# A fused attention and max-out FFN kernel: units issued from a table, state by a hardware queue, attention transposed by the DMA crossbar, token sums on two column halves

## The chip, the cores and the metric

One core of a Trainium2 chip. The metric is the device time of one execution in microseconds (us), lower is better. A program on one core has no second die to compare with, so a run counts as fast unless it is over 1.5% above the fastest run of the same kernel. In the profile PE is TensorE (matmuls), PEld its weight loads, DVE VectorE, ACT ScalarE, POOL GpSimd, SP the engine that issues hardware DMAs; SPq is SP's queue.

## The reference, cut to what matters

```python
# x: (B=8, H=8, S=512, D=64), state: (8, 8, 32, 64)
scores  = x @ state^T / 8 ;  a  = softmax(scores)  ; xread = a  @ state    # 512 tokens read the state
scores2 = state @ x^T / 8 ;  a2 = softmax(scores2) ; sread = a2 @ x        # 32 state rows read the tokens
z = concat([xread, sread], tokens) as (8*544, 512)
h = max(z@w1, z@w2, z@w3)                                                  # 512 -> 768, three ways
out = h @ w_out                                                            # 768 -> 512
```

## The kernel before: the parts that matter

All matmuls are bf16. The 512-token part never forms `xread`: a *pm unit* `m_unit(b, m)` multiplies the state of batch b into 128 columns of the three weights, and an *up* multiplies that product by the transposed attention aT. Each engine works through its instructions in the order in which they are issued, and that order is written by hand.

```python
def m_unit(b, m, eng0, eng1):       # a "pm unit": 8 matmuls in 64-row x 32-column tiles, 2 PSUM banks
    for hp in range(4):
        for par in range(2):
            mm(pm[par][hp*32:(hp+1)*32, 0:384], sbd[r0:r0+64, b, hp, par, :],
               W[r0:r0+64, :, hp, m*128:(m+1)*128], True, True, pos=(r0, hp*32))
    ...                             # two copies out of PSUM, engines eng0 and eng1
def permute_x(b, eng, ...):         # x in the order that the transposes need ("xn")
    ...
    if b >= 2:                      # from batch 2 on, the DMA crossbar transposes x ("xT")
        nc.sync.dma_start_transpose(out=xT, in_=xn)
def a_to_T(b, ...):                 # attention transposed on TensorE, copied out by DVE ("aT")
    ...
def state_reads(b):                 # sread; 16 matmuls of x, then the token sums
    ...
    for par in range(2):
        for j in range(4):
            mm(pd, ones_h[:, par, :], e[:, j, par, :, :], False, par == 1 and j == 3)  # 128 columns, half zero

# opening: idle matmuls (warm the clock), state, batches 0 to 2 - a hand-written list of calls
# then seven passes; pass t makes the outputs of one batch, the ups of the next,
# and (in the first five) scores, reads and aT of the one after it:
for what in 2 * "o u o u u M A u o u o u u M A u u M".split():   # o output half, u up, M pm unit, A attention
    ...
```

The loads go out on POOL's software queue, which casts f32 to bf16: state, x0, W[0:256], x1, W[256:512], and then, in two later groups, the rest.

The softmax here doesn't subtract the row's maximum and nothing guards it: scores larger than these inputs give would overflow.

## Time and profile before

| | before |
|---|---|
| median of 4 runs | 180.21 us (179.22 to 180.93) |
| span of the profiled run | 178.3 us, mean granted clock 0.971 |
| opening, up to the first output half of pass 1 | 57.9 us |
| five passes with attention | 86.0 us |
| the pass of the state rows | 13.05 us |
| last batch and the end | 21.4 us |

The boundaries are read from TensorE's timeline: a pass starts with its first output half (`po`). In the time-ordered chain of waits of the kernel before (start, duration, what):

```profile
31.25 1.90 POOL xn L121
33.17 14.81 DMA xT<-xn
48.03 0.64 PE ps L134 x16
```

x of batch 2 is permuted, crosses the crossbar in 14.8 us, and only then do its scores start. While it crosses, the loads of later batches run on the other queue. The DMA view of that stretch (38 to 45 us) gives packets, MB and share per queue, q0 being the loads and q1 the crossing:

```profile
q0 software_dynamic: 1607, 0.81, 87.2%
q1 hardware_dynamic: 1608, 0.41, 48.8%
```

The packet counts are nearly equal (1607 and 1608), which fits queues that take turns packet by packet; the packets of the crossing are half as large (0.41 MB against 0.81).

### The profile page before, as it was taken

What the parts mean: (1) busy time and instruction counts of PE and PEld (TensorE: products, weight loads), DVE (VectorE), ACT (ScalarE), POOL (GpSimd) and SP (SyncE); (2) the same over time, 40 slices, a digit from 0 to 9 for tenths busy, and PEclk for the clock granted to TensorE, in tenths of its full rate; (3) what the DMA queues carried; (4) which work ended last, traced back from release to release, by engine and by line L of the source; (5) the groups of instructions that cost most, each with busy time, mean ns of one, the idle gap of its engine ahead of it and who ended that gap; (6) DMA issues with size and microseconds to landing.
All of it is one profiled execution on the core that took longest, in us unless ns stands there. A gap on an engine that the chain in (4) does not pass through costs nothing.

```text
span 178.3 us, 3585 instructions
## 1 busy us (share of the span) xinstructions
PE 161.5 (91%) x1399; PEld 77.9 (44%) x1423; DVE 110.2 (62%) x195; ACT 98.4 (55%) x197; POOL 43.6 (24%) x47
## 2 busy tenths in 40 slices
PE   7958894999499999999999999999999999999880
PEld 2433452235235445444544454445444557754330
DVE  3258888388455459756975686668576764347800
ACT  2244673473446576577566847684767552444240
POOL 7909547400071062006200710170022000000000
PEclk9996999699969999999999999999999999999999
DMA  3999999999917326202620352053302022034032
GB/s 58 146 187 198 194 205 198 197 189 172 90 75 161 122 118 121 118 0 118 121 118 0 133 106 119 4 165 74 121 0 118 16 106 118 0 132 106 1 148 89
DMA packets 29473, 19.89 MB, mean 112 GB/s; under 512 B 13200, under 2 KB 26768, under 8 KB 29456
## 3 DMA queue, kind: packets, MB, share of 16 engines
q0 software_dynamic: 14000, 7.60, 32.0%
q1 hardware_dynamic: 15456, 12.06, 23.2%
q8 instruction: 11, 0.18, 0.4%
q14 instruction: 6, 0.05, 0.1%
HBM read 15.20 MB, written 8.91 MB: 135 GB/s over the span
## 4 chain that ended last, share of the span: by engine, by line
PE 65%; DMA 19%; DVE 5%; POOL 4%; issue 2%; ACT 1%; DVEq 0%; POOLq 0%
PE pw L134 28%; PE po L134 24%; DMA x_sb<-in_x_dram 11%; DMA xT<-xn 8%; PE pm L134 5%; PE pr L134 3%; PE ps L134 2%; DVE t L281 2%; PE pa L137 2%; POOL W L84 1%; POOL xn L121 1%; POOL a L233 1%; DVE ht L284 1%; PE px L137 1%; ACT xT L167 1%
## 5 line engine op out<-in xcount | busy, mean ns | idle before, releaser
L134 PE MATMUL pw<-aT,M_sb 128*128 128x512 bf16 x269 | 74.7, 388 | 3.4 <-DVE aT L207 2.3
L134 PE MATMUL po<-wout,ht 128*128 128x512 bf16 x200 | 54.6, 386 | 1.1 <-DVE ht L284 0.5
L281 DVE TENSOR_TENSOR t<-t,pw 128x512 bf16<-128x512 bf16 (+1 forms) x54 | 34.8, 644 | 22.4 <-PE pw L134 14.5
L167 ACT CAST M_sb<-pm 128x384 bf16<-128x384 f32 x88 | 38.0, 485 | 18.7 <-PE pm L134 18.7
L278 ACT CAST t<-pw 128x512 bf16<-128x512 f32 (+1 forms) x54 | 30.6, 566 | 22.8 <-PE pw L134 19.6
L134 PEld LDWEIGHTS <-M_sb 128*128 128x128 bf16 x288 | 26.9, 100 | 33.5 <-issue 4.8
L284 DVE TENSOR_TENSOR ht<-t,pw 128x512 bf16<-128x512 bf16 (+1 forms) x54 | 35.5, 658 | 7.6 <-PE pw L134 2.7
L233 POOL TENSOR_TENSOR a<-e,rden 128x512 bf16<-128x512 bf16 x16 | 16.6, 1041 | 91.5 <-DVE rden L232 91.5
L310 ACT COPY o<-po 128x512 f32<-128x512 f32 x33 | 19.4, 586 | 21.9 <-PE po L134 20.2
L134 PEld LDWEIGHTS <-ht 128*128 128x128 bf16 x204 | 18.9, 99 | 22.1 <-issue 3.2
L229 DVE TENSOR_REDUCE den<-e 128x16 f32<-128x512 bf16 x16 | 10.8, 675 | 14.5 <-ACT e L225 14.5
L134 PE MATMUL pm<-W,sbd 64*32 64x384 bf16 x384 | 17.3, 351 | 0.4 <-DMA W<-in_moe_w_dram 0.4
L134 PEld LDWEIGHTS <-sbd 64*32 64x32 bf16 x384 | 5.3, 90 | 18.9 <-issue 18.8
L121 POOL COPY xn<-x_sb 128x2048 bf16<-128x2048 bf16 x6 | 11.3, 1890 | 1.0 <-DMA x_sb<-in_x_dram 1.0
L225 ACT ACTIVATE e<-ps 128x512 bf16<-128x512 f32 x16 | 9.7, 612 | 2.2 <-PE ps L134 2.2
L134 PE MATMUL ps<-sbd,xT 128*128 128x64 bf16 x128 | 6.3, 194 | 3.8 <-DMA xT<-xn 2.3
L134 PE MATMUL pw<-AT,W 128*128 128x256 bf16 x72 | 9.2, 273 | 0.1
L253 DVE RECIPROCAL rd<-pr 128x128 f32<-128x128 f32 x8 | 7.6, 950 | 2.4 <-PE pr L134 1.8
L134 PE MATMUL pz<-zeros 128*128 128x512 bf16 x26 | 7.8, 448 | 1.2 <-DVE zeros L73 1.2
L134 PEld LDWEIGHTS <-W 128*128 128x128 bf16 x72 | 7.1, 98 | 2.5
L207 DVE COPY aT<-pa 128x1024 bf16<-128x1024 bf16 (+1 forms) x9 | 5.7, 631 | 3.4 <-PE pa L137 3.4
L134 PEld LDWEIGHTS <-xT 128*128 128x128 bf16 x128 | 4.6, 98 | 6.4 <-DMA xT<-xn 2.5
(37 smaller groups left out, 75.8 us busy)
## 6 DMA issues: line engine op xcount, KB each, us to landing
out_dram<-o SPq DMA_DIRECT2D x14, 512.0 KB, 2.6
x_sb<-in_x_dram POOLq DMA_DIRECT2D x8, 512.0 KB, 12.6
W<-in_moe_w_dram POOLq DMA_DIRECT2D x9, 256.0 KB, 7.8
out_dram<-o SPq DMA_DIRECT2D x4, 256.0 KB, 2.0
wout<-in_moe_w_out_dram POOLq DMA_DIRECT2D x1, 768.0 KB, 11.3
out_dram<-o SPq DMA_DIRECT2D x8, 64.0 KB, 1.7
st<-in_state_dram POOLq DMA_DIRECT2D x1, 256.0 KB, 3.8
xT<-xn SPq DMA_TRANSPOSE x6, 5.3
```

Source lines behind the costliest of these rows:

```text
L121: eng.tensor_copy(out=x_nat[b][:, k * n:(k + 1) * n], in_=x_sb[:, b, :, k * n:(k + 1) * n].rearrange("p h j d -> p j h d"))
L134: nc.tensor.matmul(out_ap, lhsT, rhs, start=start, stop=stop, tile_position=pos)
L167: nc.scalar.copy(out=o, in_=i)
L207: nc.vector.tensor_copy(out=d["aT"][:, :, j0 * 128:j1 * 128], in_=pa)
L225: nc.scalar.activation(out=e.rearrange("p j a hp n -> p (j a hp n)"), in_=ps.rearrange("p j a hp n -> p (j a hp n)"), func=AF.Exp, scale=s ...
L229: nc.vector.reduce_sum(out=den, in_=ef, axis=AX.X)
L233: nc.gpsimd.tensor_mul(out=d["a"][:, j0:j0 + 2].rearrange("p j a hp n -> p (j a hp) n"), in0=ef, in1=rden.unsqueeze(2).to_broadcast((128, ...
L253: nc.vector.reciprocal(out=rd, in_=pd.rearrange("p (hp n) -> p hp n", hp=HP))
L278: nc.scalar.copy(out=t[:, :nn], in_=pw[:, :nn])
L281: nc.vector.tensor_max(t[:, :nn], hts[g, "t"][:, :nn], pw[:, :nn])
L284: nc.vector.tensor_max(hts[g][:, m, :nn], hts[g, "t"][:, :nn], pw[:, :nn])
L310: nc.scalar.copy(out=o[:, j % 2, :], in_=po)
```

## The change

Its intent: fewer stalls of TensorE in the opening, and less work for TensorE in the passes. The core of the diff, cut:

```diff
+OPENING = """
+id, idle 9, sel, idle 9, lx 0, lw 0 1, lx 1, pm 0 0 v, lw 4 6, pm 0 1 g, lw 1 2, ...
+... u 0 1 0, pm 2 - g, aT 1 - v, xb 2, u 0 1 1, ... u 1 4 0, lx 7, pm 3 - g, u 1 1 0,
+lx 6, u 1 0 1, ... xb 3, u 1 4 2, ... u 1 5 1, lx 4, u 1 5 2, o 0 0 0 a, o 0 0 1 a, u 1 2 1, S 2 1 g,
+S 2 0 g, ab 2, u 1 3 1, o 0 1 0 v, M 2 2 aa, R 1, ... R 2, lx 5
+"""       # lx/lw: loads, pm: permute x, xb/ab: crossbar of x/attention, xT/aT: the same on TensorE,
+          # S: scores, M: pm unit, u: up, o: output half, R: state reads; last letters: engine
+PERIOD = "o o u u u u S S o o M M m u R u o u o X u u u u u u u P u u o u o u m M M"
-    nc.gpsimd.dma_start(out=st16, in_=state)              # software queue, casts
+    nc.sync.dma_start(out=st32, in_=state)                # hardware queue, f32
+    nc.scalar.copy(out=st16, in_=st32)
-            for j in range(J):
-                mm(pd, ones_h[:, par, :], e[:, j, par, :, :], False, par == 1 and j == J - 1)
+        for j in range(J):
+            for par in range(2):
+                mm(pd[par*64:par*64+64], ones, e[:, j, par, :, :], False, j == J - 1, pos=(0, par*64))
+    def a_crossbar(b):                                    # batches 2 to 7
+        nc.sync.dma_start_transpose(out=aT(b), in_=a_of(b))
     ...   # last tile: two half tiles, stored on two queues; outputs of the state rows moved behind the last ups
```

## The prediction

> **What bounds the kernel now.** I read the page first (engine shares, the 40 slices, the chain), then a table by stage, then the waits, then TensorE's timeline in one steady stretch.
>
> ```profile
> PE 161.5 (91%) x1399; PEld 77.9 (44%) x1423; DVE 110.2 (62%) x195; ACT 98.4 (55%) x197; POOL 43.6 (24%) x47
> ...
> PE   7958894999499999999999999999999999999880
> ...
> PEclk9996999699969999999999999999999999999999
> DMA  3999999999917326202620352053302022034032
> ```
>
> TensorE is the bound: 91% against 62% for the next engine. But the slices split the span: from slice 13 (58 us) TensorE is full at full clock; before it there are holes, three slices with the clock at 6 tenths, and saturated DMA.
>
> ```profile
> core 0: us, PE busy (x) PEld busy (x) DVE busy (x) ACT busy (x) POOL busy (x), PEclk, DMA share, GB/s
> 0.00:8.70 8.70, 7.40 (x55) 3.15 (x56) 2.81 (x7) 2.34 (x3) 7.58 (x15) 1.00 0.78 99
> 8.70:17.20 8.50, 5.66 (x84) 2.89 (x83) 5.38 (x12) 3.54 (x7) 3.79 (x6) 0.84 1.43 192
> 17.20:58.90 41.70, 35.42 (x342) 16.52 (x341) 29.14 (x52) 22.70 (x47) 14.48 (x14) 0.91 1.13 162
> 58.90:144.50 85.60, 84.86 (x766) 39.37 (x781) 59.03 (x100) 58.02 (x120) 17.77 (x14) 1.00 0.30 93
> ```
>
> I cut at the first `up` (17.2), at the end of the opening (58.9, after batch 2's aT) and at the end of the five loop passes t=1..5 that still hold attention (144.5). Those passes last 17.14 us each and TensorE is busy 84.86 of 85.60: only less TensorE work can shorten them. The opening (0 to 58.9) has idle and half clock, so order can shorten it. These waits name what holds TensorE there:
>
> ```profile
> PE pw L134 <- DVE aT L207: 2.3, 1, 2.3
> PE ps L134 <- DMA xT<-xn: 2.3, 1, 2.3
> DVE xn L121 <- DMA x_sb<-in_x_dram: 1.8, 1, 1.8
> ```
>
> Each idle of 2.3 us (28.6 to 30.9, and 45.7 to 48.0) is followed by a half-clock stretch, hence the 6s in slices 7 and 11. By the time-ordered chain, x of batch 2 lands at 31.2, is permuted by POOL (1.9 us) and crosses the crossbar in 14.8 us; the median crossing takes 5.3.
>
> Steady timeline, start first, then duration:
>
> ```profile
> 62.52 0.59 PE L134 MATMUL pw<-aT,M_sb 128*128 128x512 bf16 x2
> 62.95 0.81 PE L134 MATMUL po<-wout,ht 128*128 128x512 bf16 x3
> 63.60 1.03 PE L134 MATMUL pw<-aT,M_sb 128*128 128x512 bf16 x4
> 64.56 0.35 PE L134 MATMUL pm<-W,sbd 64*32 64x384 bf16 x8
> ...
> 69.32 0.64 PE L134 MATMUL pr<-e,xn 128*128 128x64 bf16 x16
> 69.79 0.61 PE L134 MATMUL pr<-e,ones_h 128*128 128x128 bf16 x8
> 70.24 0.59 PE L134 MATMUL pw<-aT,M_sb 128*128 128x512 bf16 x2
> ...
> 73.64 0.62 PE L137 MATMUL pa<-ident,a 128*128 128x128 bf16 x8
> 74.10 1.03 PE L134 MATMUL pw<-aT,M_sb 128*128 128x512 bf16 x3
> ```
>
> Start to start gives cost: an `up` (2 pw) 0.43, an output half (3 po) 0.65, the 16 read matmuls 0.47, the token sums (ones_h) 0.45, the aT transposes 0.46. Four pw ahead of a pm unit take 0.96 instead of 0.86: about 0.10 is lost on entering the 64*32 tiling. A pm unit itself is 0.29, a scores half 0.25. Sum of a pass: 18 up 7.8 + 8 halves 5.2 + 6 pm 1.7 + 2 scores 0.5 + reads and sums 0.92 + aT 0.46 + 6 entries 0.6 = 17.2, against 17.14 measured. So nothing but work is left there.
>
> **What the Trainium skill says.** (1) "TensorE: Matmul & The Clock Gate", Part 1: an activity monitor gates the clock to half after an idle window of about 3.4 us. The trace agrees in kind: a 2.3 us hole is enough, and the stretch from 30 to 35 us ran at 0.66. (2) "TensorEngine Tiling (Array Packing)", Key Properties: "Mode switching requires drain". The 0.10 us above agrees. (3) "DMA: Bandwidth & Descriptors", Queues, rings and completion order: a DMA engine takes turns between queue rows by packet. That fits 14.8 us against 5.3 for the crossing that ran beside the loads. (4) Same page, SWDGE vs HWDGE vs iDMA: casts need the GpSimd path, transposes the SP or ACT path. So the state, moved to SP, arrives as f32 and needs a cast (st16, on ACT).
>
> **The change part by part.**
> - *Attention through the crossbar, batches 2 to 7.* It removes 8 transposes per batch: 0.46 us of TensorE each, all on the bound, and a DVE copy (128x1024, 0.69) that is mostly hidden. Added are six crossbar transfers of half the size of xT. In the loop these have room: I estimate a lands some 5 us into a pass and aT by 10, while it is read from 16 on.
> - *Token sums on two halves.* Still 8 matmuls of 128 columns per batch, but in pairs on the two column halves: 0.45 to about 0.25, less 0.05 to 0.10 for a new mode switch. Worth 0.1 to 0.2 a batch.
> - *Loop order.* The pm units now stand in two groups of three instead of six alone: 2 entries instead of 6, -0.4. Against it, three units want six PSUM banks of eight at once and about 2 us of ACT evictions while TensorE makes them in 0.9; some stall may come back. Pass: 17.14 - 0.46 - 0.15 - 0.4 + 0.2 (estimated stall) = 16.3. Five passes: 81.5 for 85.6.
> - *Head.* State on SP frees POOL of a 0.74 us issue ahead of x(0); x(0) should land near 8.5 instead of 9.2.
> - *Opening order.* Loads: x2 behind W alone is 9.96 MB of reads in before's order (state 0.52, x0 and x1 2.10, W 4.72, wout 1.57, x2 1.05), landing at 31.2, so about 0.366 MB per us with 4 us of start and latency. In the new order x2 has 8.39 MB: 26.5. W columns 512-767 (lw 4 6) have 4.98 MB: 17.5. The second unit after the first `up` needs them, so TensorE runs densely from about 17.5. Work from there by the costs above: 36 up 15.5, 8 halves 5.2, 15 pm 4.4, 3 scores halves 0.8, 2 reads 1.5, one aT 0.5, some 12 entries 1.2: 29 us, so 46.5 with no stall. DVE has about 26 us of work in it (24 maxima at 0.73, 2 reads at 1.55, sums and copies), so it is nearly as full and will leave gaps. I add 2.5 us: opening ends at 49.0 instead of 58.9.
> - *State stretch (157.4 - 144.5 = 12.9):* same work, 12.8.
> - *End.* After the last maxima DVE paces (1.39 per block against 1.29 on TensorE) and TensorE sat 1.0 us at 168; state outputs moved behind the last ups fill that, -0.9. The two halves of the last tile were copied one after the other (0.37, 0.42); now separate tiles on two queues, -0.5. 20.9 becomes 19.5.
>
> Sum: 49.0 + 81.5 + 12.8 + 19.5 = 162.8 us span; before, 180.06 was measured for a span of 178.3, so add 1.8: **164.6 us**.
>
> **The rivals.**
> 1. *Crossing waits at the joint.* xT of batch 2 now starts near 28.5 but still beside loads until about 42; if it takes 14 us again it lands at 42.5, while TensorE reaches those scores near 38 to 40. Then aT of batch 2 must cross too (before: on TensorE) and the first pass needs it at once. For it: 14.8 us in the trace, all loads still queued. Against: the scores stand late in the table. Opening ends at 52 to 53, perhaps with one clock dip: 168 to 169.
> 2. *Evictions become the bound in the loop.* Three pm units at a stretch stall on ACT; the pass stays near 16.9: +3 us, 167.5. Against it: ACT is busy 58 of 85.6 and DVE 59, and DVE loses the aT copy.
> 3. *It goes fully to plan.* No dip, no gap: opening 46.5, pass 16.0: 160.5.
> 4. *The opening is bound by loads and gains little:* 57, then 172.5. Against: after 35 us TensorE had everything it needed except xT.
>
> **Range and chances.** Rivals 1 and 2 pull up, 3 down: 161.0 to 170.0 eight times in ten. Being within 2% needs over 176.5, so an opening without gain and a loop with half of its own: 0.04. Slower: 0.01.
>
> **What would show it.** Right: TensorE work per pass 16.0 to 16.5 us with PE busy over 97% of it; no pa after batch 1; clock lows in the opening one or none; x(0) landed by 8.6; first pass begins at 47 to 51; TensorE idle at the end under 0.5 us ahead of the last outputs. Wrong: a wait of TensorE on xT or aT of batch 2 over 2 us, pm units waiting for ACT or DVE in every pass, or a half-clock stretch after 50 us. Of the saving of 15.5 I expect 9.9 in the opening, 4.1 in the passes and 1.5 after them.

## The result, and the profile after

The changed kernel takes **168.68 us** (median of 4 runs, 167.81 to 170.32) against 180.21. The ratio is 0.937 (95% interval 0.929 to 0.946). Ratios here and below are the mean time of one kernel's fast runs over that of the other's in the same rounds, so not quite the ratio of the medians. That is inside the predicted range, 4.1 us above the point.

The profiled run is the slowest of the four, 170.32 us with a span of 168.5. Where it lost its 1.6 us against the median has a likely place: x of batch 2 was there to be permuted at 28.3 us, and at 26.9 and 27.0 in e3 and e11 below, which have the same code up to there. By the same boundaries (the last stage of the changed kernel begins with an up, because its outputs of the state rows were moved):

| | before | predicted saving | after | saving |
|---|---|---|---|---|
| opening | 57.9 | 9.9 | 56.5 | 1.4 |
| five passes | 86.0 | 4.1 | 79.6 | 6.4 |
| state rows | 13.05 | 0.1 | 13.05 | 0 |
| last batch and end | 21.4 | 1.4 | 19.4 | 1.9 |

The predicted sum came near, but not by its terms: the passes gave more than promised, the opening nearly nothing. The page of the changed kernel:

```profile
PE 151.6 (90%) x1353; PEld 74.9 (44%) x1370; DVE 109.0 (65%) x194; ACT 92.9 (55%) x190; POOL 46.7 (28%) x50
...
PE   7958999990299989999999999999999999999991
...
PEclk9999999998559999999999999999999999999997
```

The many small holes of the opening are gone. Slices 9 and 10 (counted from 0) hold one large hole, and slices 10 to 12 a stretch at half clock, 10 us from 40.5 to 50.8. TensorE's timeline there, and the matching piece of the chain:

```profile
37.09 0.59 PE L105 MATMUL pw<-aT,M_sb 128*128 128x512 bf16 x2
45.17 1.03 PE L105 MATMUL ps<-sbd,xT 128*128 128x64 bf16 x16 [7.48 <-DMA xT<-xn]
```

```profile
30.24 14.89 DMA xT<-xn
```

So x of batch 2 starts to cross 2.9 us earlier than before, takes as long as before, and TensorE is now at its scores at 37.7 instead of 45.7. What the faster order saved ahead of that point it spent waiting for one transfer. The crossing shares the engines with the loads from 36 to 45 us (q0 the loads), while a crossing in a pass has them to itself (99 to 103 us):

```profile
q0 software_dynamic: 1573, 0.80, 83.4%
q1 hardware_dynamic: 1639, 0.41, 62.5%
```

```profile
xT<-xn SPq DMA_TRANSPOSE x1, 3.7
```

The last number is microseconds from issue to landing: 3.7 alone, against 14.9 beside the loads.

In the passes (table by stage of the changed kernel, one steady pass, columns as in the prediction's) TensorE is as full as before, and a pass takes 15.77 us instead of 17.14:

```profile
88.71:104.48 15.77, 15.66 (x155) 7.47 (x149) 12.05 (x22) 10.58 (x23) 3.88 (x3) 1.00 0.44 117
```

Its timeline shows what three pm units in a row cost, and the reads and sums:

```profile
72.32 0.68 PE L105 MATMUL pm<-W,sbd 64*32 64x384 bf16 x24
72.94 1.47 PE L105 MATMUL po<-wout,ht 128*128 128x512 bf16 x5
...
78.88 0.63 PE L105 MATMUL pr<-e,xn 128*128 128x64 bf16 x16
79.44 0.41 PE L105 MATMUL pr<-e,ones 128*64 128x128 bf16 x8
79.79 0.60 PE L105 MATMUL pw<-aT,M_sb 128*128 128x512 bf16 x2
```

Start to start, three units take 0.62 us, 0.207 each; alone each took 0.285 and delayed what came before it by 0.10. The reads now take 0.56 (0.47 before) and the sums 0.35 (0.45): together 0.91, before 0.92.

### The profile page after: what moved, and what is told of

It reads as the page before. It is cut to its first block, busy times and chain, and to the rows that moved or that the text cites. A ratio compares the mean times of both kernels' runs of the same rounds, so it can differ in the third digit from the quotient of the medians.

```text
span 168.5 us, 3476 instructions
## 1 busy us (share of the span) xinstructions
PE 151.6 (90%) x1353; PEld 74.9 (44%) x1370; DVE 109.0 (65%) x194; ACT 92.9 (55%) x190; POOL 46.7 (28%) x50
## 4 chain that ended last, share of the span: by engine, by line
PE 76%; DMA 16%; POOL 4%; issue 1%; DVE 1%; ACT 1%; POOLq 0%; DVEq 0%; ACTq 0%
PE pw L105 39%; PE po L105 25%; DMA xT<-xn 9%; DMA W<-in_moe_w_dram 7%; PE pm L105 6%; PE pr L105 4%; POOL W L140 2%; PE ps L105 2%; POOL x_sb L146 1%; DVE ht L298 0%; DVE t L296 0%; ACT t L292 0%; PE pa L108 0%; DVE oh L102 0%; ACT oh L100 0%
## 5 line engine op out<-in xcount | busy, mean ns | idle before, releaser
L105 PE MATMUL pw<-aT,M_sb 128*128 128x512 bf16 x288 | 71.3, 381 | 0.1
L105 PE MATMUL po<-wout,ht 128*128 128x512 bf16 x189 | 50.9, 384 | 1.0 <-issue 0.3
L105 PEld LDWEIGHTS <-M_sb 128*128 128x128 bf16 x288 | 26.5, 98 | 32.5 <-issue 3.7
L100 ACT CAST M_sb<-pm 128x384 bf16<-128x384 f32 x81 | 33.2, 504 | 5.3 <-PE pm L105 5.3
L238 POOL TENSOR_TENSOR a<-e,rden 128x512 bf16<-128x512 bf16 x14 | 14.4, 1044 | 73.0 <-ACT e L230 46.8
L102 POOL COPY xn<-x_sb 128x2048 bf16<-128x2048 bf16 (+1 forms) x9 | 15.1, 1687 | 7.4 <-DMA x_sb<-in_x_dram 7.2
L105 PE MATMUL pm<-W,sbd 64*32 64x384 bf16 x384 | 12.7, 331 | 0.6 <-DVE ht L298 0.4
L105 PEld LDWEIGHTS <-sbd 64*32 64x32 bf16 x384 | 4.3, 90 | 10.9 <-issue 10.2
L140 POOL DMA_DIRECT2D W<-in_moe_w_dram x12 | 9.0, 766 | 0.0
L102 DVE CAST M_sb<-pm 128x384 bf16<-128x384 f32 x15 | 7.8, 529 | 1.3 <-PE pm L105 1.3
L105 PE MATMUL pz<-zeros 128*128 128x512 bf16 x20 | 6.9, 495 | 1.2 <-DVE zeros L120 1.2
```

The costliest lines, as they stand in the source:

```text
L100: nc.scalar.copy(out=o, in_=i)
L102: ENG[eng].tensor_copy(out=o, in_=i)
L105: nc.tensor.matmul(out_ap, lhsT, rhs, start=start, stop=stop, tile_position=pos)
L140: nc.gpsimd.dma_start(out=W[:, i, :, c], in_=w_v[i][:, :, c])
L238: ENG[eng].tensor_mul(out=a_of(b)[:, 2 * h:2 * h + 2].rearrange("p j a hp n -> p (j a hp) n"), in0=e, in1=rden.unsqueeze(2).to_broadcast(( ...
```

## The experiments

Twelve kernels ran, all correct. The first three ask why the opening gained so little.

**Theory A**: TensorE waits because the crossing of x of batch 2 takes turns with the loads. **Rival B**: the opening lacks something else, and the wait only hides it.

**e1: x of batch 2 on TensorE.**

```diff
-xb 2, u 0 1 1, ...            o 0 0 1 a, u 1 2 1, S 2 1 g
+u 0 1 1, ...                  o 0 0 1 a, xT 2 0 v, xT 2 1 a, u 1 2 1, S 2 1 g
```

> The changed kernel, but x of batch 2 is transposed on TensorE (16 transposes, copies on DVE and ACT) instead of by the crossbar. Theory A (TensorE waits 7.5 us because this one crossing takes some 15 us beside the loads): the wait goes, the half-clock stretch after it goes, TensorE pays about 1 us; 162 to 164 us. Rival B (the opening is short of something else too, evictions or loads, and the crossing only hides it): another wait of some us appears in its place, 167 to 169 us.

Measured: 164.3 us (163.91 to 164.75), ratio to before 0.912. The wait is gone and 4.4 us with it, after about 0.9 us of transposes that TensorE now does. A second wait shows that was not seen before, at the joint to pass 1:

```profile
51.41 1.90 PE L105 MATMUL pw<-aT,M_sb 128*128 128x512 bf16 x8 [1.57 <-DMA aT<-a]
```

The attention of batch 2 crosses beside the last loads too. A holds; B holds only in this small part.

**e2: the loads of x4 to x7 at the end of the opening.**

```diff
-lx 7, ... lx 6, ... lx 4, ... R 2, lx 5
+... R 2, lx 4, lx 7, lx 6, lx 5
```

> The changed kernel, but the loads of x for batches 4 to 7 are issued at the end of the opening, so that only x3 and W_out are still moving when x of batch 2 crosses. Theory A1 (the crossing is slow because it takes turns with the loads): it lands within 5 to 8 us of its issue, TensorE waits under 1 us for it; about 163 us unless the later crossing of the attention of batch 2 then collides. Rival A2 (it is slow by itself, as the first of two crossings): still 12 us or more, the wait stays at 5 us or more and the time at 167 to 169 us.

Measured: 162.94 us (162.2 to 163.69), ratio 0.904. The crossings are the same two, but the loads are out of their way. The DMA view from 29 to 38 us:

```profile
q1 hardware_dynamic: 2603, 0.66, 88.0%
q0 software_dynamic: 646, 0.63, 43.0%
...
xT<-xn SPq DMA_TRANSPOSE x2, 7.8
```

The 7.8 us are the mean of two: the crossing of batch 2, which the scores need, lands after 9.3 us, and the second after 6.4. So 5 to 8 us was missed for the one that counts. It lands at 38.6, just when the scores begin (38.58): their weight load waits 1.3 us for it, TensorE itself 0.8. Theory A1 holds in the main: the same crossing takes 9.3 us instead of 14.9 when fewer loads move beside it, and the long wait goes. The later crossing of aT still costs a wait of 1.5 us.

**e3: x of batch 3 is meant to cross only after the scores of batch 2.**

```diff
-xb 3, u 1 4 2, ...    S 2 0 g, ab 2
+u 1 4 2, ...          S 2 0 g, xb 3, ab 2
```

> The changed kernel, but x of batch 3 crosses only after the scores of batch 2, so that one crossing alone stands beside the loads. If the second crossing slows the first: x of batch 2 lands 3 us or more earlier and the time falls to about 165. If the loads alone do it (theory A1): it still lands 13 to 15 us after its issue, and the time stays at 167 to 169 us.

Measured: 168.59 us (168.52 to 168.74), the time of the changed kernel. But the edit did not do what it was meant to do. SP works through its own instructions in order, and for SP that order is the same with and without the edit: crossing of x2, of x3, of the attention of batch 2. Nothing makes the crossing of x3 wait for scores. In the trace both crossings are under way long before the scores, the second issued at 33.41 (changed kernel first, then e3):

```profile
30.24 15.06 SPq L212 DMA_TRANSPOSE xT<-xn  x2
28.76 14.54 SPq L212 DMA_TRANSPOSE xT<-xn  x2
```

So e3 is the changed kernel run once more, and its expectation came true without being tested. The first crossing was issued at 28.76 and the scores began at 43.41:

```profile
43.41 1.03 PE L105 MATMUL ps<-sbd,xT 128*128 128x64 bf16 x16 [6.16 <-DMA xT<-xn]
```

That is again 14.6 us. What does settle the question are two other traces in which one crossing alone stands beside the loads: x of batch 2 in the kernel before took 14.8 us (the next crossing was issued at 54.26), and x of batch 3 in e4 took 14.7 (issued at 31.36). A second crossing is not needed for the delay; the loads are.

**e4: both transposes of batch 2 on TensorE.** As e1, and:

```diff
-S 2 0 g, ab 2, u 1 3 1, ...  R 2, lx 5
+S 2 0 g, u 1 3 1, ...        R 2, aT 2 - v, lx 5
```

> As e1, and the attention of batch 2 is transposed on TensorE as well (8 transposes, copy on DVE), so that nothing of the opening but x of batch 3 crosses. Theory A with a second wait at the joint to the first pass: 0.5 to 1.5 us below e1, 161 to 163 us. If the crossing of the attention is hidden in e1: same as e1 or 0.5 us above it.

Measured: **161.8 us** (161.65 to 162.23), ratio 0.898. It beats both kernels, and no other version tried was faster. Pass 1 starts at 47.9 us instead of 56.5, and the clock stays at 1.0. It is the base of most that follows, because its runs spread by 0.6 us where those of the changed kernel spread by 2.5.

**e5: attention of the passes back on TensorE.**

```diff
-                a_crossbar(nb)
+                a_array(nb, None, "v")
```

> From e4 (161.8 us) with this one part undone: the attention of batches 3 to 7 is transposed on TensorE with a DVE copy, as before the change. Theory (TensorE is the bound in the loop): a pass gets 0.46 us longer, five passes 2.3 us, so 164 us. Rival (the evictions of the new loop order bind, DVE has no room for the copy): 1 us a pass or more, 167 us.

Measured: 164.48 us (164.27 to 164.7). A pass takes 16.21 us instead of 15.77:

```profile
64.50:80.71 16.21, 16.21 (x157) 7.89 (x156) 12.63 (x22) 10.57 (x23) 3.87 (x3) 1.00 0.31 98
```

The part is worth 0.44 us a pass, 2.2 in five; 2.7 were measured in all.

**e6: the pm units one by one again.**

```diff
-o o u u u u S S o o M M m u R u o u o X u u u u u u u P u u o u o u m M M
+o o u u M u u u S S o o M u m R u o u o X u u u m u u u u P M u u o u M o u
```

> From e4 with the six pm units of a pass standing alone again, other work between any two. Theory from the trace of the changed kernel (three in a row cost 0.71 us with entry, alone 0.39 each with entry and exit): 0.9 us a pass more, so 4.4 us in five passes, 166 us. The prediction's size (0.4 less 0.2 of stalls given back): 1 to 2 us in all, 163 to 164. Rival (order does not matter, PSUM evictions do): no change or faster.

Measured: 166.79 us (166.28 to 167.0), 5.0 us more. TensorE has no idle time in such a pass, and it is 0.92 us longer:

```profile
65.11:81.80 16.69, 16.69 (x150) 7.29 (x149) 12.04 (x21) 10.67 (x23) 3.88 (x3) 1.00 0.40 111
```

Same matmuls, same busy time on DVE and ACT, more time on TensorE: what grows is the number of changes of tiling. Six visits to the 64*32 tiling against two are four more, at 0.23 us each.

**e7: token sums over all columns, with a zero-padded ones matrix.**

```diff
-                mm(pd[par*64:par*64+64], ones, e[:, j, par, :, :], False, j == J-1, pos=(0, par*64))
+                mm(pd, ones[:, par, :], e[:, j, par, :, :], False, par == 1 and j == J-1)
```

> From e4 with the token sums over all 128 columns against a zero-padded ones matrix, as before the change. From the trace (reads and sums 0.91 us against 0.92 before): no difference over 0.3 us, 161.8. The prediction's size (0.1 to 0.2 us for each of 8 batches): 162.6 to 163.4.

Measured: 162.45 us (162.09 to 162.67), 0.65 above e4, but not where the sums are. A pass is as long as with the halves:

```profile
65.23:80.99 15.76, 15.76 (x156) 7.60 (x148) 12.05 (x22) 10.57 (x23) 3.88 (x3) 1.00 0.46 117
```

In the profiled runs the two kernels are already 0.77 us apart at 18 us, where TensorE waits for a load of W. e5, e6 and e12, which keep e4's opening, start there at 18.07, 17.59 and 19.02, so 0.77 in one trace tells nothing, and what puts the medians 0.65 apart is open. In the passes the part is worth nothing.

**e8: the opening in the order of the kernel before.** The table of e4 replaced by the calls of the old opening, with their engines:

```diff
-id, idle 9, sel, idle 9, lx 0, lw 0 1, lx 1, ...
+id, lx 0, lw 0 2, lx 1, lw 2 4, idle 10, sel, idle 14, pm 0 0 v, pm 0 1 v, xT 0 0 v, xT 0 1 a, S 0 0 g, ...
```

> From e4 with the units of the opening in the order and with the engines of the kernel before (x of batch 2 by the crossbar after the loads are queued, attention of batch 2 on TensorE), the rest as in the changed kernel. If order is worth what the prediction said (9 to 10 us): 171 to 172 us. If the order of the table gains little by itself: under 166 us.

Measured: 167.53, 170.71, 170.88 and 170.99 us. By the 1.5% rule only the first counts as fast, so there is no interval, and which of the two levels is the usual one is not settled. Against the one fast run the table is worth 5.7 us (167.53 - 161.8). In that run pass 1 starts at 53.8 us; in e4 at 47.9. So the order gains something near 6 us, less than the 9 to 10 of the expectation, unless the upper level is the usual one (then 9.0). In the changed kernel the wait for one crossing (7.5 us) took that back. Of the 10 us between the kernel before (57.9) and e4 some 4 are then not the table's; e9 finds 1.6 of them in the loading of the state, and the rest was not tested.

**e9: the state by POOL's queue again.** From e4:

```diff
-    nc.sync.dma_start(out=st32, in_=state);   nc.scalar.copy(out=st16, in_=st32)
+    nc.gpsimd.dma_start(out=st16, in_=state)
```

> From e4 (161.8 us) with the state loaded as before the change: by POOL's queue with a cast on the way, no f32 copy on ACT. The prediction's size: x of batch 0 lands 0.7 us later, 162.5. Rival from the traces (the changed kernel's first copy of x began between 8.3 and 9.5 us in five runs, against 9.2 before, so the earlier issue is partly lost to the state's own f32 transfer ahead of it): under 0.5 us, 161.8 to 162.3.

Measured: 163.61 us (162.71 to 163.85, 6 runs), 1.8 above e4 and 1.6 above e12, which has e4's head and ran in the same rounds (161.98). The part is worth more than either size expected. In the profiled run the first copy of x begins late:

```profile
9.45 0.43 DVE L102 COPY xn<-x_sb 128x1024 bf16<-128x1024 bf16 x1 [1.71 <-DMA x_sb<-in_x_dram]
```

With the state on SP that copy began at 8.3 to 9.5 us in six profiled runs (the changed kernel, e1 to e4, e12), so one trace can't tell how much of the 1.6 us it is. The same holds where TensorE next waits for a load, for W behind the first `up`: it goes on at 19.35 us in e9 and at 17.78 in e4, but at 17.59 to 19.02 over ten profiled runs with the state on SP. Where the 1.6 us arise stays open.

**e10: the kernel before, with the pm units of a pass in two groups of three and nothing else.**

```diff
-2 * "o u o u u M A u o u o u u M A u u M"
+2 * "o u o u u M M M A u o u o u u A u u"
```

> The kernel before with one part of the change alone: in the loop, the pm units stand in two groups of three instead of six alone. Theory (entering and leaving the 64*32 tiling costs 0.2 us each time): a pass falls from 17.14 to about 16.2, 175.6 to 176.2 us in all. Rival (all evictions of pm are on ACT here, so three in a row stall for PSUM): 177.5 to 180.

Measured: 177.8 us (177.24 to 178.86), ratio 0.988 (0.984 to 0.991), a gain clear of the noise. A pass falls from 17.14 to 16.59, 0.55 and not 0.9. By start times the grouping itself saves about 0.87 (six times 0.385 against two times 0.72), but each pass now waits for a bank:

```profile
69.75 0.63 PE L134 MATMUL pr<-e,xn 128*128 128x64 bf16 x16 [0.24 <-DVE t L281]
```

So both views held in part: six banks at once do bite in the old order, and the new order, with its other places for scores and outputs, avoids it.

**e11: zero matmuls in front of the wait.** From the changed kernel:

```diff
-u 1 2 1, S 2 1 g
+u 1 2 1, idle 26, S 2 1 g
```

> The changed kernel (168.7 us) with 26 matmuls of zeros, 5.6 us of work at full clock, ahead of the scores of batch 2, where TensorE waits for the crossing. They cannot shorten the wait. If half of the loss is the half-clock stretch after it: the clock stays at 1.0 and the time falls by 2 to 3 us, to 166. If the wait alone costs: no change, 168.7, or longer.

Measured: 168.99 us (167.95 to 169.86), against 168.68: no gain, although the clock stayed at 0.99 to 1.0. The half-clock stretch, which looks costly on the page, was nearly free; of its 10 us, 4.6 lay inside the wait, where TensorE had nothing to do. TensorE's timeline shows why:

```profile
42.91 0.63 PE L105 MATMUL ps<-sbd,xT 128*128 128x64 bf16 x16
...
54.83 1.90 PE L105 MATMUL pw<-aT,M_sb 128*128 128x512 bf16 x8 [1.64 <-DMA aT<-a]
```

From the scores to the first `up` of pass 1 it takes 11.9 us at full clock, and it took 12.6 in the changed kernel (45.17 to 57.77) at half clock for much of it. That stretch is set by another chain: scores, exponentials, POOL's product, and then the crossing of aT beside the loads. The crossing was issued 4.3 us after the scores in e11 and 4.5 in the changed kernel, and took 7.5 in both. My expectation of 2 to 3 us fell. These are two traces; the runs spread by 2 us, so a gain under 1 us can't be excluded by the times alone.

**e12: the last output tile in two PSUM banks.** From e4: each half of its columns is accumulated in its own bank and copied and stored by itself.

```diff
-                copy("av"[k], o, po[:, f])
+                pk = bank([128, half], F32, "pk")
+                for kt in range(MT):
+                    mm(pk, ht[:, kt, j*128:(j+1)*128], wout[:, kt, f], kt == 0, kt == MT - 1)
+                copy("av"[k], o, pk)
```

> From e4 (161.8 us) with the last output tile made in two PSUM banks of 256 columns, so that its two copies no longer share a bank: in the changed kernel the copy on DVE still began only after that on ACT. Theory: the first half leaves while the second is computed, 0.3 to 0.5 us less, 161.4. Rival: the last transfer's own latency hides it, no change.

Measured: 161.98 us (161.69 to 162.69) against 161.8. No gain. The DVE copy no longer waits for ACT's, and it doesn't matter.

## Why the prediction was right or wrong

- **The bound.** Right. TensorE is 99% busy in a steady pass before and after, and the two parts that took work from it there, the crossbar (0.44 us) and the grouping (0.92), nearly add up to the 1.37 us by which a pass fell.
- **Crossbar for the attention in the passes, 0.46 us a pass.** Right: 0.44 by e5. As estimated, the crossing is hidden there.
- **Loop order, 0.4 a pass less 0.2 of stalls given back.** The mechanism was right, the size was not. I counted only the 0.10 us lost on entering the 64*32 tiling. Leaving it costs about as much, hidden in the 0.285 us of a unit standing alone, which I booked as work. Measured: 0.92 a pass (e6), with no stall in a steady pass. Rival 2 (evictions become the bound) fell for this order, as TensorE has next to no idle in a pass; e10 shows that it would not have been empty in the old one.
- **Token sums, 0.1 to 0.2 a batch.** The sums did fall by 0.10, but the reads ahead of them grew by 0.09: the switch of tiling gave the whole gain back. Worth nothing in a pass (e7).
- **Passes.** A saving of 4.1 predicted, 6.4 measured: a steady pass 15.77 instead of 16.3, and the first one 16.5.
- **Head.** I expected x0 by 8.6. It varied from 8.3 to 9.5 with the same code. By the measured time of e9 the part is worth about 1.6 us, more than the 0.7 that I gave it.
- **Opening, 49.0 instead of 58.9.** This is the step that failed: 9.9 us of saving predicted, 1.4 measured. Its term "I add 2.5 us" for all stalls was mis-sized: one wait alone was 7.5 us in the profiled run, and pass 1 began at 56.5. By the boundary of the table above, 48.0 was promised. The working of rival 1 named that wait, both numbers that make it (a crossing of 14 us beside the loads, TensorE there at 38 to 40) and its total of 168 to 169; I set it aside because the scores stand late in the table. They stood at 37.7, and the crossing landed at 45; a wait of over 2 us on xT was also my own sign of being wrong, and it came. But rival 1 put the end of the opening at 52 to 53, and by the prediction's boundary (the first `up` of pass 1) it came at 57.8, so that its total fits is luck too. One sum of the step held a slip: 8.39 MB at 0.366 MB per us and 4 us more is 26.9 us, not 26.5, for x of batch 2 to land; it was there at 28.3 in the profiled run. The rest of the step was sound: with the two crossings of batch 2 taken out (e4), which costs TensorE some 1.3 us for the transposes, pass 1 begins at 47.9. Rival 4 (the opening bound by its loads) was true only by way of these crossings.
- **The clock dip in rival 1.** It came, and by the traces of e11 and the changed kernel it cost about 0.7 us (12.6 against 11.9), because another crossing was the next thing to be waited for.
- **End, 1.4.** Measured 1.9. The hole ahead of the last outputs closed as expected. The copies of the last tile still run one after the other (the DVE copy of the second half begins at 165.21, after ACT's), so the reason that I gave for the other 0.5 was wrong, and e12 shows that parting them is worth nothing. From the end of the last matmul to the end of the span it takes 3.7 us instead of 5.0. Only the smaller last transfers, on two queues, are left to explain it; that was not tested by itself.

The sum came out within range by luck: two errors had opposite signs. In savings, and for the profiled run: 2.8 us too little for the passes and the end, 8.5 too much for the opening.

## What to carry to other kernels

When an order is tightened, ask of each transfer how long it takes *beside the traffic of that moment*, not in the median: the consumer moves earlier, the transfer doesn't, and the gain becomes a wait. In this kernel, while the loads saturate DMA, the transposes are cheaper on TensorE, even though it is the bound (e4: 6.9 us less than the changed kernel); once the loads are done, the crossing is hidden (e5). And stand matmuls of one tiling next to each other: here the cost came per visit to the other tiling (0.23 us), on entering and on leaving. Last, when an experiment moves an instruction, look in the trace whether it moved: an order written in one list is no order between engines (e3).

## What the Trainium skill lacked or had wrong

- "TensorEngine Tiling (Array Packing)", Key Properties, says that a mode switch drains TensorE, but gives no size. Here a visit to the 64*32 tiling among 128*128 matmuls costs 0.23 us beyond its work (four visits more: 0.92 us a pass).
- The same page, Theoretical Speedup, gives up to 2x for a dimension of 64. For 8 matmuls of 128 columns among full-size ones the gain was none (15.77 against 15.76 us a pass): at this size the switch eats it.
- "DMA: Bandwidth & Descriptors", DMA Transpose (X-bar), has no figure for a crossing beside loads. Here the same transpose of a 128x2048 bf16 tile took 14.9 us beside a saturated load queue and 3.7 us alone, with nearly equal packet counts on the two queues. The page's rule (Rules for kernel authors) that a transpose next to ordinary DMAs needs nothing is about correctness; it says nothing of this cost.
- "TensorE: Matmul & The Clock Gate", Why this matters for your kernels, asks for no idle gaps over some 3 us. Here gaps of 2.3 us were enough for a half-clock stretch (before). One of 1.54 us in e1 was followed by half clock too (from about 11.3 to 14.7 us), and one of 1.71 in the changed kernel was not: length alone did not decide. A stretch of 10 us at half clock, 4.6 of it inside the wait, cost about 0.7 us by the traces (e11).
